# Three half decays at other places in the order of a recurrent attention and mixture kernel, and a gate transpose in four column tiles

## The chip, the cores and the metric

One core of a Trainium2 chip runs the whole program. The metric is the device time of one execution in microseconds (us), taken as the median of several runs. The engines are TensorE (PE in the profile, with PEld for its weight loads), VectorE (DVE), ScalarE (ACT), GpSimd (POOL) and SyncE (SP), which issues the DMAs.

## The reference

A gated recurrent attention (mLSTM) over 2 batches, 8 heads, 768 steps and 40 features, followed by a dense mixture of 4 experts over the 1536 tokens:

```python
m_new = np.maximum(f_gate[:, :, t] + m, i_gate[:, :, t])
f_stab = np.exp(f_gate[:, :, t] + m - m_new)
i_stab = np.exp(i_gate[:, :, t] - m_new)
C = f_stab[:, :, None, None] * C + i_stab[:, :, None, None] * np.einsum('bhd,bhe->bhde', vt, kt)
n = f_stab[:, :, None] * n + i_stab[:, :, None] * kt
h_tilde = np.einsum('bhde,bhe->bhd', C, qt)
nq = np.einsum('bhd,bhd->bh', n, qt)[:, :, None]
y[:, :, t] = sigmoid(o_gate) * h_tilde / np.maximum(np.abs(nq), 1.0)
...
p = domain_probs / (domain_probs.sum(-1, keepdims=True) + 1e-09)
h = np.maximum(x @ w1[e], 0.0)
out += p[:, e:e + 1] * (h @ w2[e])
```

Here x is y with the heads side by side: 320 features for each token. The hidden size is 1024.

## The kernel before

The recurrence is computed in 12 chunks of 128 tokens. Chunk n belongs to batch n % 2 and to position n // 2 of 6. For each chunk the kernel makes score products of keys and queries (`scores`, PE, line L473), weighs them with a matrix of decays (`weigh`, DVE, L479), multiplies with the values (`intra`, PE, L535), adds what the carried state gives (`inter`, PE, L520), normalises (`norm`, DVE, L548 to L555) and transposes the result into the experts' input (`turn`, PE, L562; `turn_lo`, DVE, L573 and L574). `state` (PE, L491) with the additions of L501 (DVE) and `carry` (POOL, L507) bring the state to the next chunk of the batch. `values` (POOL, L456) and `keys` (POOL, L462) scale values and keys; keys needs both halves of the chunk's decays.

`decay(n, i)` (L438) makes half i (4 heads) of the decay matrix of chunk n by one scan on DVE (L442). For chunks 0 to 3 its input fb lies in PSUM, where `spread` put it; from chunk 4 on fb is loaded into SBUF by DMA (`load_f`). Its second input, id4, always lies in SBUF.

The engines run their instructions in the order in which the program issues them, which is written out by hand (manual_schedule). The loop over chunks (L722) issues, for chunk n: state(n), turn_lo(n-1), inter(n+1), intra(n), norm(n), scores(n+1), values, keys, weigh and carry of n+1, and then the steps of `PLAN[n]` (L38): D is the next half of decay n+2, Hjk two hidden tiles of the first expert for 256 tokens (8 times 2 products, L164, then a relu: L207 on ACT for the rounded part, L208 on DVE for the rest), Ojk a quarter of the output products (L224), T the transpose. In chunk 3 the program also issues the last split of the second weight matrix (`split_w2`: L104 on ACT, L107 on POOL), a reciprocal (L761, DVE) and the product of the expert weights with it (L762, POOL), all between carry(4) and the first step of PLAN[3].

The score products and the state and transpose products share the two PSUM buffers of the pool `ps_w`. A new pair of score buffers is free when the state additions (L501) and turn_lo (L573, L574) have read the tiles there before.

`gate_t` (L346) turns the input gates, 48 rows by 128 tokens for each chunk position, to tokens in partitions, with one fp32 product of the whole array for each of the 6 positions (L353): one position early, five later, followed by an ACT copy (L357). An fp32 product shows up as two matrix instructions.

After the 12 chunks the experts run in tiles of 512 tokens, with nothing but products, relus and accumulation.

Of the kernel before, what the change touches and what calls it, by code (L numbers as in the profile page):

```python
# [15 lines left out]
B, H, S, D = 2, 8, 768, 40  # L16
NE, DM, FF = 4, 320, 1024
NT = B * S
L = 128
# [16 lines left out]
NPE = 4  # L36

PLAN = {  # L38
    2: "D H03 D O00 T",
    3: "D O01 D O02 T",  # L40
    4: "D H10 D H11 O03 T",
    5: "D H12 D H13 O10 T",
    6: "D O11 H20 D H21 T",
    7: "D O12 D O13 O20 T",
    8: "D H22 D H23 O21 T",
    9: "D O22 H30 D H31 T",
    10: "O23 H32 H33 O30 T",
    11: "O31 O32 T O33",
}
PAD = 56  # L50

NB = 4
W = 512
# [3 lines left out]
def tile_mlstm_moe(ctx, tc, gt, qk, vk, ot, dp, w1, w2, out):  # L57
    ctx.enter_context(tc.manual_schedule())
    nc = tc.nc

    def pool(name, bufs, **kw):
        return ctx.enter_context(tc.tile_pool(name=name, bufs=bufs, **kw))
# [4 lines left out]
    hps = []  # L67
    pool("pad", 1, side="right").tile([L, PAD], F32, name="pad")
    dram = pool("dram", 1, space=DRAM)
# [58 lines left out]
    def load_w1e(e):  # L128
        raw1 = raws.tile([L, 3, FF], F32, tag="raw", name="raw1")
        nc.sync.dma_start(raw1, w1[e])  # L130
        return raw1
# [111 lines left out]
    with ExitStack() as actx:  # L243
# [40 lines left out]
        ib = gp.tile([L, S], F32, name="ib")  # L284
        fr = a1.tile([L, NPE // B * L], F32R, name="fr")
        f_d = dram.tile([BH, S], F32, name="f_d")
        ident = const.tile([L, L], F32, name="ident")
# [58 lines left out]
        def gate_t(c0, c1):  # L346

            pit = pits[c0] = ps_y.tile([L, 512], F32, tag="y", name="pit")
            n = c1 - c0
            po = n * 48  # L350
            for c in range(c0, c1):
                o = (c - c0) * 48
                nc.tensor.matmul(  # L353
                    pit[:, o:o + 48], ib[:, c * L:(c + 1) * L], ident[:, 0:48],
                    start=True, stop=True,
                )
            nc.scalar.activation(  # L357
                ibT[:, c0:c1], pit[:, 0:po].rearrange("t (c g) -> t c g", c=n), AF.Copy
            )
# [38 lines left out]
        def load_qk(j, c=None):  # L398
            c = slice(0, 2) if c is None else slice(c, c + 1)
            nc.sync.dma_start(qks[j % 2][:, c], qk[j, :, c])  # L400

        def load_vk(j, c=None):
            if j not in vks:
                vks[j] = a2.tile([L, 2, 2, H, D], F32, tag="vk", name="vk")
            c = slice(0, 2) if c is None else slice(c, c + 1)
            nc.sync.dma_start(vks[j][:, c], vk[j, :, c])

        def load_o(j):
            nc.sync.dma_start(acc[:, 2 * j:2 * j + 2], ot[:, 2 * j:2 * j + 2])

        def gate_o(j):
            og = acc[:, 2 * j:2 * j + 2]
            nc.scalar.activation(og, og, AF.Sigmoid)  # L413
# [15 lines left out]
        def load_f(n, fb=None):  # L429
            b, c = n % B, n // B  # L430
            if fb is None:
                fb = a0.tile([L, H, L], F32, tag=f"fb{n % 2}", name="fb")
            fbs[n] = fb[:, 0:4], fb[:, 4:8]
            nc.sync.dma_start(
                fb, f_d[b * H:(b + 1) * H, c * L:(c + 1) * L].unsqueeze(0).to_broadcast([L, H, L])
            )

        def decay(n, i=None):  # L438
            if i != 1:
                dds[n] = a1.tile([L, H, L], F32, tag=f"dd{n % 2}", name="dd")  # L440
            for i in range(2) if i is None else (i,):
                nc.vector.tensor_tensor_scan(  # L442
                    out=dds[n][:, 4 * i:4 * i + 4].rearrange("p h t -> p (h t)"),
                    data0=fbs[n][i].rearrange("p h t -> p (h t)"),
                    data1=id4.rearrange("p h t -> p (h t)"),
                    initial=0.0, op0=ALU.mult, op1=ALU.add,
                )

        def values(n, part=None):
            b, c = n % B, n // B  # L450
            vv = vvs[n] = vp[n % 2]
            iec = ibT[:, c, b * H:(b + 1) * H].unsqueeze(2)
            if part != LO:
                nc.scalar.activation(vv[:, :, D:D + 1], iec, AF.Copy)
            if part != HI:
                nc.gpsimd.tensor_mul(  # L456
                    vv[:, :, 0:D], vks[n // 2][:, n % 2, 0], iec.to_broadcast([L, H, D])
                )

        def keys(n):  # L460
            if n // B < NC - 1:
                nc.gpsimd.tensor_mul(  # L462
                    kp[n % 2], vks[n // 2][:, n % 2, 1],
                    dds[n][:, :, L - 1:L].to_broadcast([L, H, D]),
                )
# [9 lines left out]
        def weigh(n):  # L475
            pms[n] = a1.tile([L, H, L], F32, tag=f"pm{n % 2}", name="pm")
            pm, dd = (t.rearrange("k (p r) t -> k r p t", r=2) for t in (pms[n], dds[n]))
            for r in range(2):
                nc.vector.tensor_mul(pm[:, r], ss[n][r], dd[:, r])  # L479

        def state(n, pool=ps_w, tag="w"):

            b, c, vv, kk = n % B, n // B, vvs[n], kp[n % 2]
            if c == NC - 1:
                return
            st = pool.tile([L, NP, L], F32, tag=tag, name="st")
            blocks = [(slice(64 * r, 64 * r + D), slice(64 * r, 64 * r + D + 1)) for r in range(2)]
            for p in range(NP):
                for r, (q, q2) in enumerate(blocks):
                    h = 2 * p + r  # L490
                    nc.tensor.matmul(  # L491
                        st[q, p, q2], kk[:, h], vv[:, h, 0:D + 1], start=True, stop=True
                    )
            cout = cs[b]
            if c == 0:
                for q, q2 in blocks:
                    copy(nc.scalar, cout[q, :, q2], st[q, :, q2])
            else:
                cd = cds.pop(n)
                for q, q2 in blocks:  # L500
                    nc.vector.tensor_add(cout[q, :, q2], cd[q, :, q2], st[q, :, q2])  # L501
# [29 lines left out]
        def intra(n):  # L531
            y = y0s[n] = ps_y.tile([L, H, 64], F32, tag="y", name="y0")
            for h in range(H):
                for t in (slice(0, 64), slice(64, L)):
                    nc.tensor.matmul(  # L535
                        y[t, h, 0:D + 1], pms[n][:, h, t], vvs[n][:, h, 0:D + 1],
                        start=True, stop=True,
                    )
# [32 lines left out]
        def turn_lo(n):  # L571
            px, t = pxs.pop(n), slice(n * L, (n + 1) * L)
            nc.vector.tensor_sub(xst[:, 3:5, t], px[:, 0:2], xst[:, 0:2, t].bitcast(F32))  # L573
            nc.vector.tensor_sub(xst[C:L, 2, t], px[0:C, 2], xst[0:C, 2, t].bitcast(F32))  # L574
# [147 lines left out]
        for n in range(2, NCH):  # L722
            j, cc = n // 2, n % 2
            plan = PLAN[n].split()
            nxt = n + 1 < NCH
            if cc == 0 and 2 < j + 1 < NG:
                load_qk(j + 1)
                load_vk(j + 1)
            if n > 3 and n + 3 < NCH:
                load_f(n + 3)  # L730
            if cc == 0:
                if j > 1:
                    gate_o(j)
                if j + 1 < NG:
                    load_o(j + 1)
            if n == NCH - 2:
                raw1 = load_w1e(1)
            state(n)
            if n > 2:
                turn_lo(n - 1)  # L740
            if nxt:
                inter(n + 1)
            intra(n)
            norm(n)
            if nxt:
                scores(n + 1)
            for a in plan:
                if a[0] == "H":
                    work[int(a[1])].corners(int(a[2]) // 2 * 4)
                    break  # L750
            if nxt:
                values(n + 1)
                keys(n + 1)
                weigh(n + 1)
                carry(n + 1)
            if n == 2:
                split_w2_lo(w2s, 4, 2, w2r, nc.gpsimd)
            if n == 3:
                split_w2(w2s, 6, 2, w2r, nc.gpsimd)
            if n == 3:  # L760
                nc.vector.reciprocal(psum_e, psum_e)  # L761
                nc.gpsimd.tensor_mul(pw, pw, psum_e.to_broadcast([L, NCH, NE]))  # L762
            half = 0
            for a in plan:
                if a == "T":
                    turn(n, ps_w, "w")
                    turn_d(n, n + 1)
                elif a == "D":
                    decay(n + 2, half)
                    half = 1  # L770
                else:
                    step(a)
# [103 lines left out]
```

## Time and profile before

| | us |
|---|---|
| median of 3 runs | 402.92 (402.8 to 402.92) |
| profiled execution | 402.67 |
| its span | 400.9 |
| PE busy | 395.2 (99%) |
| DVE busy | 172.6 (43%) |
| ACT busy | 127.7 (32%) |
| POOL busy | 81.0 (20%) |

The granted clock of TensorE is at full speed in every slice of the span. A row of a timeline gives the start of an instruction or of a run of equal instructions, its length, engine, line, operation, output and inputs, and in brackets the idle time of the engine before it with what ended it. Consecutive instructions of DVE and POOL overlap a little in the records, so the distance from one start to the next is shorter than the length. The chunks end at about 116 us; the rest of the span is expert work.

### The profile page before, as it was taken

The numbers are of one execution on the slowest core, as the hardware profiler recorded it, in microseconds if no ns is written. First come the engines' busy times: TensorE is split into PE (matmuls) and PEld (weight loads), VectorE is DVE, ScalarE is ACT, GpSimd is POOL, SyncE is SP. The second block draws the span as 40 slices with busy tenths as digits, with TensorE's granted clock in tenths as the row PEclk, the third lists the DMA queues.
The fourth block names the chain that finished last, engine by engine and source line by source line (L and its number), as shares of the span: only waits on it lengthen the run. The fifth ranks groups of instructions, "written<-read, shape, count | busy, mean of one in ns | idle before, by whom it ended". The sixth has DMA issues, their size and how long they took to land.

```text
span 400.9 us, 7146 instructions
## 1 busy us (share of the span) xinstructions
PE 395.2 (99%) x3044; PEld 359.0 (90%) x3044; DVE 172.6 (43%) x313; ACT 127.7 (32%) x309; POOL 81.0 (20%) x93
## 2 busy tenths in 40 slices
PE   9899999999999999999999999999999999999996
PEld 6798999999988988988989989989889889899896
DVE  8878987878534124123133153142241341331321
ACT  4776344444526333016021051061130320220310
POOL 4888622310007110007100010043100100000000
PEclk9999999999999999999999999999999999999999
DMA  6999564670000304000300022003000001001001
GB/s 170 333 299 284 171 156 135 159 289 2 2 0 2 131 2 157 2 0 5 128 0 2 0 70 88 2 1 132 0 0 2 1 2 49 18 14 37 17 18 49
DMA packets 15000, 29.34 MB, mean 73 GB/s; under 512 B 1000, under 2 KB 10760, under 8 KB 13656
## 3 DMA queue, kind: packets, MB, share of 16 engines
q1 hardware_dynamic: 14968, 28.88, 22.7%
q8 instruction: 24, 0.39, 0.4%
q14 instruction: 8, 0.07, 0.1%
HBM read 26.86 MB, written 2.02 MB: 72 GB/s over the span
## 4 chain that ended last, share of the span: by engine, by line
PE 93%; DVE 3%; ACT 2%; POOL 1%; issue 1%; DMA 1%; DVEq 0%; POOLq 0%
PE ph L164 42%; PE po L224 42%; PE s L473 3%; PE y L535 2%; PE y L520 1%; PE px L562 1%; PE st L491 1%; DMA gat<-in_gt 1%; DVE mb L302 0%; PE fb L423 0%; POOL fs L310 0%; ACT yb L527 0%; ACT acc L413 0%; POOL fs L311 0%; POOL ib L321 0%
## 5 line engine op out<-in xcount | busy, mean ns | idle before, releaser
L164 PE MATMUL ph<-xst,w1s 128*128 128x512 f32 (+3 forms) x840 | 174.0, 363 | 0.0
L224 PE MATMUL po<-w2s,h 128*128 128x320 f32 x1152 | 173.2, 310 | 0.0
L224 PEld LDWEIGHTS po<-w2s,h 128*128 128x128 f32 x1152 | 169.8, 188 | 1.5
L164 PEld LDWEIGHTS ph<-xst,w1s 128*128 128x128 f32 (+1 forms) x840 | 141.0, 189 | 28.0 <-issue 4.2
L207 ACT ACTIVATE h<-ph 128x512 fp32r<-128x512 f32 x96 | 57.3, 598 | 198.1 <-PE ph L164 198.1
L208 DVE SCALAR_TENSOR_TENSOR h<-ph,h 128x512 fp32r<-128x512 f32 x96 | 66.1, 689 | 103.4 <-ACT h L207 102.8
L234 DVE SCALAR_TENSOR_TENSOR acc<-po,pw,acc 128x320 f32<-128x320 f32 x36 | 19.8, 551 | 99.9 <-PE po L224 99.9
L107 POOL TENSOR_TENSOR w1s<-raw,w1s 128x512 fp32r<-128x512 f32 (+1 forms) x24 | 23.6, 1023 | 96.7 <-ACT w1s L104 96.7
L107 POOL TENSOR_TENSOR w2s<-raw,w2s 128x640 fp32r<-128x640 f32 x6 | 9.5, 1577 | 98.2 <-ACT w2s L104 98.2
L442 DVE TENSOR_TENSOR_SCAN dd<-fb,id 128x512 f32<-128x512 f32 x22 | 25.9, 1204 | 0.0
L527 ACT ACTIVATE yb<-y,ibT 128x41 f32<-128x41 f32 x80 | 15.9, 316 | 1.0 <-DVE cs L501 0.5
L164 PE MATMUL ph<-xd,w1s 64*128 64x512 f32 (+1 forms) x56 | 15.9, 391 | 0.0
L473 PE MATMUL s<-qk 64*128 64x128 f32 (+1 forms) x192 | 14.9, 284 | 0.5 <-DVE cs L501 0.3
L479 DVE TENSOR_TENSOR pm<-s,dd 128x512 f32<-128x512 f32 x24 | 15.3, 679 | 0.0
L473 PEld LDWEIGHTS s<-qk 64*128 64x128 f32 (+1 forms) x192 | 12.4, 187 | 2.0 <-issue 0.7
L104 ACT ACTIVATE w2s<-raw 128x640 fp32r<-128x640 f32 x12 | 8.8, 734 | 16.6 <-DMA raw<-in_w 16.6
L535 PE MATMUL y<-vp,pm 128*64 128x41 f32 x384 | 13.3, 229 | 0.5 <-POOL vp L456 0.3
L535 PEld LDWEIGHTS y<-vp,pm 128*64 128x64 f32 x384 | 12.6, 138 | 1.0 <-POOL vp L456 0.4
L456 POOL TENSOR_TENSOR vp<-vk,ibT 128x320 f32<-128x320 f32 x12 | 10.5, 876 | 12.7 <-PE y L535 9.5
L462 POOL TENSOR_TENSOR kp<-vk,dd 128x320 f32<-128x320 f32 x10 | 7.3, 736 | 23.7 <-DVE dd L442 23.7
L104 ACT ACTIVATE w1s<-raw 128x512 fp32r<-128x512 f32 (+1 forms) x24 | 11.2, 517 | 0.0
L232 ACT ACTIVATE acc<-po,pw 128x320 f32<-128x320 f32 x12 | 6.3, 528 | 15.1 <-PE po L224 15.1
(86 smaller groups left out, 186.0 us busy)
## 6 DMA issues: line engine op xcount, KB each, us to landing
raw<-in_w SPq DMA_DIRECT2D x3, 1536.0 KB, 9.8
raw<-in_w SPq DMA_DIRECT2D x3, 1280.0 KB, 5.4
fb<-f_d SPq DMA_DIRECT2D x7, 512.0 KB, 4.9
qk<-in_qk SPq DMA_DIRECT2D x4, 832.0 KB
vk<-in_vk SPq DMA_DIRECT2D x5, 640.0 KB, 10.2
acc<-in_ot SPq DMA_DIRECT2D x6, 320.0 KB, 9.5
out<-acc SPq DMA_DIRECT2D x12, 160.0 KB, 1.8
qk<-in_qk SPq DMA_DIRECT2D x4, 416.0 KB
```

The source lines that it names most:

```text
L104: nc.scalar.activation(hi, raw, AF.Copy)
L107: eng.tensor_sub(lo, raw, hi.bitcast(F32))
L164: nc.tensor.matmul(self.banks[i][:, f % self.nf, :], self.w1s[r, wi, f * L:(f + 1) * L], x[r, self.t0:self.t0 + self.n], start=(i not in s ...
L207: nc.scalar.activation(hh, ph, AF.Relu)
L208: nc.vector.scalar_tensor_tensor(out=hl, in0=ph, scalar=0.0, in1=hh.bitcast(F32), op0=ALU.max, op1=ALU.subtract)
L224: nc.tensor.matmul(po, self.hs[f][a][:, sl], ws[:, b, f, :], start=(first and i == 0), stop=(last and i == len(ks) - 1),)
L234: nc.vector.scalar_tensor_tensor(out=acc[:, i, :], in0=po, scalar=pw[:, i, e:e + 1], in1=acc[:, i, :], op0=ALU.mult, op1=ALU.add,)
L442: nc.vector.tensor_tensor_scan(out=dds[n][:, 4 * i:4 * i + 4].rearrange("p h t -> p (h t)"), data0=fbs[n][i].rearrange("p h t -> p (h t)") ...
L473: nc.tensor.matmul(ss[n][r][:, p, :], kg[q, p], qg[q, p], start=True, stop=True)
L479: nc.vector.tensor_mul(pm[:, r], ss[n][r], dd[:, r])
L527: nc.scalar.activation(yb[:, h], y1[:, h, 0:D + 1], AF.Copy, scale=ibT[:, c, i:i + 1])
L535: nc.tensor.matmul(y[t, h, 0:D + 1], pms[n][:, h, t], vvs[n][:, h, 0:D + 1], start=True, stop=True,)
```

## The change

The second half of the decay of chunk 4 is issued in chunk 3, between values(4) and keys(4), instead of in chunk 2. The second halves of chunks 8 and 11 are issued ahead of a hidden step (H20, H30) instead of after it. Each of the six products of gate_t becomes four, with 32 tokens each, that write 32 partitions of the result.

```diff
 PLAN = {
-    2: "D H03 D O00 T",
+    2: "D H03 O00 T",
...
-    6: "D O11 H20 D H21 T",
+    6: "D O11 D H20 H21 T",
...
-    9: "D O22 H30 D H31 T",
+    9: "D O22 D H30 H31 T",
...
+QUADS = [slice(i, i + 32) for i in range(0, L, 32)]
...
-                nc.tensor.matmul(
-                    pit[:, o:o + 48], ib[:, c * L:(c + 1) * L], ident[:, 0:48],
-                    start=True, stop=True,
-                )
+                for t in QUADS:
+                    nc.tensor.matmul(
+                        pit[t, o:o + 48], ib[:, c * L + t.start:c * L + t.stop],
+                        ident[:, 0:48], start=True, stop=True,
+                    )
...
                 values(n + 1)
+                if n == 3:
+                    decay(4, 1)
                 keys(n + 1)
```

## Rows read from the trace of the kernel before

**Rows 1.** The page, section 1: busy time, share of span, instructions of each engine.
```profile
PE 395.2 (99%) x3044; PEld 359.0 (90%) x3044; DVE 172.6 (43%) x313; ACT 127.7 (32%) x309; POOL 81.0 (20%) x93
```
**Rows 2.** The chain that ended last, in order of time: start us, us, what.
```profile
38.62 0.30 DVE xst L574
38.91 0.04 issue
38.95 1.16 PE s L473 x14
```
**Rows 3.** Timeline of PE, chunks 3 and 4.
```profile
35.84 0.51 PE L491 MATMUL st<-vp,kp 128*40 128x41 f32 x16
36.92 1.08 PE L535 MATMUL y<-vp,pm 128*64 128x41 f32 x32
...
45.16 1.08 PE L535 MATMUL y<-vp,pm 128*64 128x41 f32 x32
46.17 1.16 PE L473 MATMUL s<-qk 64*128 64x128 f32 x16
```
**Rows 4.** Timeline of DVE over the same stretch.
```profile
34.59 1.28 DVE L442 TENSOR_TENSOR_SCAN dd<-acc,id 128x512 f32<-128x512 f32 x1
...
36.38 1.21 DVE L442 TENSOR_TENSOR_SCAN dd<-acc,id 128x512 f32<-128x512 f32 x1
37.51 0.64 DVE L501 TENSOR_TENSOR cs<-cd,st 40x164 f32<-40x164 f32 x2
...
38.62 0.28 DVE L574 TENSOR_TENSOR xst<-px,xst 64x128 fp32r<-64x128 f32 x1
38.82 0.49 DVE L548 TENSOR_TENSOR y<-y,yb 128x328 f32<-128x328 f32 x1
...
40.81 1.28 DVE L479 TENSOR_TENSOR pm<-s,dd 128x512 f32<-128x512 f32 x2
...
42.14 2.31 DVE L442 TENSOR_TENSOR_SCAN dd<-fb,id 128x512 f32<-128x512 f32 x2
44.70 0.66 DVE L501 TENSOR_TENSOR cs<-cd,st 40x164 f32<-40x164 f32 x2 [0.26 <-PE st L491]
...
46.29 0.51 DVE L548 TENSOR_TENSOR y<-y,yb 128x328 f32<-128x328 f32 x1 [0.17 <-PE y L535]
```
**Rows 5.** Timeline of POOL over the same stretch.
```profile
33.21 1.59 POOL L107 TENSOR_TENSOR w2s<-w2r,w2s 128x640 fp32r<-128x640 f32 x1
34.74 1.66 POOL L456 TENSOR_TENSOR vp<-vk,ibT 128x320 f32<-128x320 f32 x1
37.73 0.74 POOL L462 TENSOR_TENSOR kp<-vk,dd 128x320 f32<-128x320 f32 x1 [1.34 <-DVE dd L442]
38.42 1.04 POOL L507 TENSOR_TENSOR cd<-cs,bl 104x512 f32<-104x512 f32 x1
39.52 1.56 POOL L107 TENSOR_TENSOR w2s<-w2r,w2s 128x640 fp32r<-128x640 f32 x1
42.30 1.06 POOL L762 TENSOR_TENSOR pw<-pw,psum_e 128x48 f32<-128x48 f32 x1 [1.22 <-DVE psum_e L761]
43.33 1.63 POOL L456 TENSOR_TENSOR vp<-vk,ibT 128x320 f32<-128x320 f32 x1
```
**Rows 6.** The tile vp, its products on POOL: length ns min/median/max.
```profile
L456 POOL TENSOR_TENSOR vp<-vk,ibT x12: 712/722/1655, 10.7 to 92.1; 128x320 f32<-128x320 f32 x12
```
**Rows 7.** Timeline of DVE: two halves of a decay in chunk 7, with POOL idle.
```profile
76.84 2.33 DVE L442 TENSOR_TENSOR_SCAN dd<-fb,id 128x512 f32<-128x512 f32 x2
```
**Rows 8.** Timelines of PE, DVE and ACT around the end of chunk 6.
```profile
73.37 1.57 PE L473 MATMUL s<-qk 64*128 64x128 f32 x16
...
71.74 0.67 DVE L208 SCALAR_TENSOR_TENSOR h<-ph,h 128x512 fp32r<-128x512 f32 x1
...
71.06 0.60 ACT L207 ACTIVATE h<-ph 128x512 fp32r<-128x512 f32 x1 [1.08 <-PE ph L164]
```
**Rows 9.** The chain that ended last: pieces of small fp32 products, with their counts.
```profile
22.82 0.74 PE st L491 x32
...
24.60 1.10 PE pit L353 x10
...
45.33 0.91 PE y L535 x32
```

## The prediction

> **What bounds the kernel now.** I read first the busy table of the page: PE is busy for 99% of the span [rows 1], so an edit pays only where it removes a PE gap or PE work, and costs where it makes PE wait. Next the chain that ended last. It is PE almost everywhere from 17 us on, except for one stretch up to 38.95 us that runs through DVE: there the score products of chunk 4 (PE, L473) wait for the second turn_lo subtraction of chunk 2 (DVE, L574) [rows 2]. Last I read the timelines of PE, DVE and POOL around that place, row by row, since an edit that moves DVE work must be followed there.
>
> The size of that gap: the y products (L535) of chunk 3 start at 36.92. In the next chunk the scores start 1.01 us after the y products (45.16 to 46.17) [rows 3], so these could start at 37.93. Their second product starts at 38.95. PE loses 1.02 us. The reason is on DVE [rows 4]: the second half of decay 4 runs from 36.38 to 37.59, then come the state additions (37.51) and turn_lo (to 38.90), and only then are both score buffers of ps_w free.
>
> One chunk on, PE does not wait, but only just: DVE ends turn_lo(3) a moment before the scores of chunk 5 start at 46.17. DVE is idle there for 0.26 us (before 44.70) and 0.17 us (before 46.29) [rows 3, 4]. So DVE between 34.59 and 46.3 has about 0.4 us to spare in all, and a DVE instruction of 1.13 us that is moved inside that stretch can't vanish.
>
> **Part 1, decay(4,1) moved from chunk 2 to chunk 3.** It leaves the place after H03's relu and stands between norm(3) and weigh(4). It issues no DMA. Removed: DVE goes from 36.38 straight to the state additions, which must wait for PE's state products (35.84 + 0.51 = 36.35), so about 36.45; additions and turn_lo take 1.39 us (37.51 to 38.62 + 0.28) [rows 3, 4], so the buffers are free at 37.85, before PE wants them at 37.93. The gap of 1.02 us is gone, and PE reaches the scores of chunk 5 at 46.17 - 1.02 = 45.15.
>
> Added, in DVE's order: norm(3) starts when its y products are in, 36.92 + 1.13 (the lag 45.16 to 46.29) = 38.05. norm takes 1.99 (38.82 to 40.81): 40.04. The moved half: next instruction after 1.13 (36.38 to 37.51), end after 1.21: 41.17 and 41.25. weigh(4) and the reciprocal, 1.33 (40.81 to 42.14): decay(5,0) is due at 42.50. If nothing disturbs the two halves of decay 5, they take 2.31 less the 0.08 overlap: 44.73; additions and turn_lo 1.39: 46.12; the scores follow 0.05 later (38.90 to 38.95): 46.17 [rows 2 to 4]. That is exactly the old time. So even undisturbed **the 1.02 us come back as a wait one chunk later**: net 0.0 us. What is late next is the scores of chunk 5, behind cs and turn_lo.
>
> And it is disturbed, by POOL. Queued behind the new wait on POOL are keys(4), carry(4), the last low-part split of w2 (L107), the pw product (L762) and values(5). Before, keys, carry and split ran at 37.73, 38.42 and 39.52, while DVE was at norm and weigh, and POOL was idle when decay 5 began [rows 5]. Now keys(4) starts 0.14 us after the decay's end (37.59 to 37.73): 41.39; carry(4) 0.69 later: 42.08, until 43.12; the split right behind it. Carry and split now fall on the two scans of decay 5 (due 42.50).
>
> What do such neighbours cost? A scan of a chunk from 4 on has both inputs in SBUF (fb loaded by DMA, id4). Values(4) on POOL took 1.66 us and values(5) 1.63, where the median of this product is 0.72; both began during such a scan [rows 4 to 6]. Taking 0.72 off the end of the first (36.40) leaves 35.68: POOL stood still until 0.19 us before the scan's recorded end (35.87). The other way round there is one row: decay(4,0) began while the POOL split of 33.21 was running and took 1.28 instead of 1.21 [rows 4, 5]; so it began in fact 0.07 later, at 34.66, 0.14 before that split's end (34.80). A running POOL instruction holds a scan of this kind, and a running scan holds POOL. Who goes first between two scans: L762 began at 42.30, in the first scan of decay 5, and ended at 43.36, while the second scan ran until 44.45 [rows 4, 5], so a waiting POOL instruction gets in between. It was short (48 columns), and that pair took 2.31 against 2.33 for a pair with POOL idle [rows 4, 7], so this row can't show what a long one costs.
>
> The sum by this: decay(5,0) is held from 42.50 to 43.12 - 0.14 = 42.98 and ends at 44.19. The split gets in at 44.19 - 0.19 = 44.00 and takes 1.56: 45.56. decay(5,1) runs from 45.56 - 0.14 = 45.42 to 46.63. The additions start 0.08 before that, 46.55; turn_lo ends 47.94; scores at 47.99 instead of 46.17: **+1.82 us** on PE. Bounds: 0.0 if the two engines don't hold each other; +0.48 if only carry holds a scan. I take the upper end, since three POOL rows and one DVE row are lengthened by it. Afterwards PE and DVE are late by nearly the same, and in later chunks POOL waits for the decay anyway, so no second clash follows.
>
> The Trainium skill, "SBUF — State Buffer", section "Who interferes with whom", states that a DVE instruction with two SBUF inputs and a GpSimd instruction that reads SBUF take an exclusive lock, and that the second to issue is blocked for the whole instruction of the first. Here it speaks against the change: by it alone, both carry and split would hold the scans, which is the sum just made; without it the sum would be zero.
>
> **Part 2, decays 8 and 11.** The second half now runs before the relu of H20 (H30) instead of after it, in DVE time that was idle. In chunk 6 the DVE half of the H21 relu started at 71.74, but ACT's half ended only at 71.06 + 0.60 = 71.66 [rows 8]. So what follows moves up by at most 0.08, and I take 0.05. The next scores on PE, those of chunk 8, wait 0.41 us (1.57 against 1.16 for the 16) [rows 3, 8], and that wait stays nearly whole. keys(8) runs earlier on POOL while DVE has no scan. Chunk 9 shows the same pattern without a wait: 0. If the idle time were too short, the first relu would be late by a few hundredths, still under its successor.
>
> **Part 3, the gate turn.** 12 matrix pieces (two for each chunk's fp32 product) become 48, of 32 output rows each; 40 of them lie at 24.6 us, where PE has no gap. Before: 1.10 us for 10. No row has 32-column pieces. The nearest: 64-column pieces with 41 moving columns, 0.91 / 32 = 28 ns; 40-column pieces, 0.74 / 32 = 23 ns [rows 9]. At 28 ns: 40 x 28 = 1.14, a loss of 0.04. At 23: 0.92, a gain of 0.18. If four tiles overlap twice as well as two: 0.46, a gain of 0.64. I take the nearest in width, 0.18. ACT's reading of the result doesn't bind. The other 8 pieces stand in the start-up, where PE runs filler products: 0.
> The skill's page "TensorEngine Tiling (Array Packing)", section "Performance Considerations", gives some 60 cycles of overhead to each matmul; that would be an estimate of 25 ns a piece at 2.4 GHz, 1.0 us for 40, a gain of 0.1. No row here has this width.
>
> **The sum**, against the profiled execution (402.67 us, span 400.9): +1.82 - 0.05 - 0.18 = +1.59, 404.26. The median of the timed runs is 0.25 higher, 402.92, so **404.5**. What a measurement of this kernel can tell from no change is about 0.2%, 0.8 us.
>
> **The rivals.**
> A, the forecast: carry and split hold the scans. 404.5, with the bounds of the gate turn 404.0 to 404.7. For it: the lengthened rows. Against: only one DVE row is lengthened, and by 0.07 only. Chance 0.53.
> B: carry holds the first scan, but the second scan follows the first before the split gets in (DVE's next instruction is already queued). +0.48 - 0.23 = +0.25: 403.2. For it: the pair of decay 5 was not lengthened by L762. Chance 0.18.
> C, the other side: DVE is not held by POOL, POOL alone waits. Then the gap goes from the scores of chunk 4 to those of chunk 5 and the change does not do what its first edit is after; only the gate turn counts: 0.0 - 0.23: 402.7 (402.2 to 402.9). It decides as soon as decay 5 stays at 2.3 us a pair. Chance 0.22.
> D: as C, with the 32-column pieces at half of 23 ns or less, so that 0.64 or more comes off PE and the DVE chain moves up with it: about 402.1 or below. Chance 0.07; I count most of it as faster by over 0.2%.
>
> Faster by over 0.2%: 0.06; within: 0.40 (B, C, the rest of D); slower: 0.54 (A and a little of B). For 8 in 10 the range must reach into C: 402.5 to 404.9, where the upper end adds to A's 404.7 a few hundredths for each of its hand-overs; A's own is 404.0 to 404.7.
>
> **What would show it.** Right: no gap before the scores of chunk 4; a DVE pair of decay 5 that spans some 4 us instead of 2.31, with a POOL split between its halves, and a gap of nearly 3 us before the scores of chunk 5. Wrong: decay 5 at 2.3 us (C), or only its first half long (B). Part 3 is read from the start of the gate pieces to the next hidden products (1.10 before), part 2 from the scores' 1.57. The prediction falls most likely if a waiting scan is served ahead of POOL, or if POOL's order differs from the one that I read.

## The result and the profile after

The changed kernel takes 407.32 us (median of 4 runs, 406.12 to 408.79) against 402.92 for the kernel before: slower by a ratio of 1.0092, 95% interval 1.0065 to 1.0119 (that of the two medians is 1.0109). The profiled execution took 407.58 us, its span is 405.8.

The page shows the busy table with PE at 98% [rows 1], and in the line of the granted clock two slices below 9, which the kernel before does not have:

```profile
PE 398.7 (98%) x3080; PEld 361.9 (89%) x3080; DVE 175.2 (43%) x313; ACT 127.8 (31%) x309; POOL 81.1 (20%) x93
...
PEclk9999889999999999999999999999999999999999
```

PE's timeline over chunks 3 and 4 [rows 3]:

```profile
38.11 1.26 PE L475 MATMUL s<-qk 64*128 64x128 f32 x16
...
44.42 1.08 PE L537 MATMUL y<-vp,pm 128*64 128x41 f32 x32
47.77 2.32 PE L475 MATMUL s<-qk 64*128 64x128 f32 x14 [2.27 <-DVE cs L503]
...
50.86 5.14 PE L165 MATMUL ph<-xst,w1s 128*128 128x256 f32 x28
55.84 1.93 PE L225 MATMUL po<-w2s,h 128*128 128x320 f32 x12
```

The scores of chunk 4 (38.11) take 1.26 us, 0.10 more than the 1.16 of [rows 3]: their old gap is all but gone. The first score product of chunk 5 waits 2.27 us, and the others wait for turn_lo (DVE below, 48.09 + 0.28 = 48.37): the forecast gap of nearly 3 us is there. What was not forecast stands in the lengths behind that: 16 scores that took 1.16 us [rows 3] take over 2, and 28 hidden products take 5.14. In the kernel before they took 3.62:

```profile
47.50 3.62 PE L164 MATMUL ph<-xst,w1s 128*128 128x256 f32 x28
50.96 1.34 PE L224 MATMUL po<-w2s,h 128*128 128x320 f32 x8
```

DVE and POOL over the same stretch [rows 4, 5]:

```profile
40.23 1.22 DVE L444 TENSOR_TENSOR_SCAN dd<-acc,id 128x512 f32<-128x512 f32 x1
41.55 1.29 DVE L481 TENSOR_TENSOR pm<-s,dd 128x512 f32<-128x512 f32 x2
...
42.90 4.17 DVE L444 TENSOR_TENSOR_SCAN dd<-fb,id 128x512 f32<-128x512 f32 x2
46.99 0.64 DVE L503 TENSOR_TENSOR cs<-cd,st 40x164 f32<-40x164 f32 x2
...
48.09 0.28 DVE L576 TENSOR_TENSOR xst<-px,xst 64x128 fp32r<-64x128 f32 x1
```
```profile
41.59 0.74 POOL L464 TENSOR_TENSOR kp<-vk,dd 128x320 f32<-128x320 f32 x1 [4.82 <-DVE dd L444]
42.30 1.04 POOL L509 TENSOR_TENSOR cd<-cs,bl 104x512 f32<-104x512 f32 x1
43.30 1.55 POOL L108 TENSOR_TENSOR w2s<-w2r,w2s 128x640 fp32r<-128x640 f32 x1
44.80 1.19 POOL L766 TENSOR_TENSOR pw<-pw,psum_e 128x48 f32<-128x48 f32 x1
45.95 1.63 POOL L458 TENSOR_TENSOR vp<-vk,ibT 128x320 f32<-128x320 f32 x1
```

The pair of decay 5 spans 4.17 us instead of 2.31 [rows 4]. Carry and split have their usual lengths, stand together and end at 44.85, in its first half; the pw product and values(5) behind them are the stretched ones.

The stretches around the gap; the columns are the stretch, its length, the busy time of PE, PEld, DVE, ACT and POOL with the count of instructions, the granted clock, the share of the DMA engines and GB/s:

```profile
44.00:46.00 2.00, 1.50 (x46) 1.38 (x42) 2.00 (x2) 1.96 (x8) 2.00 (x3) 1.00 0.01 5
46.00:48.00 2.00, 0.23 (x1) 0.26 (x2) 1.96 (x4) 0.68 (x5) 2.00 (x2) 0.89 0.00 0
48.00:50.00 2.00, 2.00 (x16) 1.81 (x18) 1.85 (x8) 0.00 (x0) 1.95 (x3) 0.50 0.72 210
...
54.00:56.00 2.00, 2.00 (x18) 2.00 (x17) 1.11 (x2) 0.60 (x1) 0.00 (x0) 0.91 0.00 0
56.00:58.00 2.00, 2.00 (x16) 1.82 (x14) 1.36 (x2) 1.32 (x3) 1.15 (x2) 1.00 0.00 0
```

From 48 to 54 us the granted clock is 0.50, the lower of the two levels, 1.2 GHz. So the 4.9 us between the two spans are in two places. The scores of chunk 5 start at 47.77 instead of 46.17: 1.60. From there to the output products of chunk 4 (55.84; 50.96 in the kernel before, whose chain then runs on without a wait) it takes 8.07 us instead of 4.79: 3.28. All that follows is equal to 0.01 us.

The gate turn and what stands behind it, in PE's timeline, with keys(2) from POOL's:

```profile
24.91 0.63 PE L355 MATMUL pit<-ident,ib 128*32 128x48 f32 x40
25.47 1.94 PE L165 MATMUL ph<-xst,w1s 128*128 128x256 f32 x14
...
28.81 0.51 PE L493 MATMUL st<-vp,kp 128*40 128x41 f32 x16
```
```profile
28.02 0.74 POOL L464 TENSOR_TENSOR kp<-vk,dd 128x320 f32<-128x320 f32 x1
```

From the first gate piece to the next hidden products it is now 0.56 us for 40 pieces, 14 ns a piece. The state products of chunk 2 then start at 28.81, right at the end of keys(2) (28.76); in the kernel before they started at 28.72. This execution had begun its hidden products later (17.98 against 17.62); counted from there, 0.27 us of the saving is left at the state products (10.83 us against 11.10), but on the time line nothing is.

The wait before the scores of chunk 8 is 0.03 us shorter than in [rows 8]:

```profile
78.25 1.54 PE L475 MATMUL s<-qk 64*128 64x128 f32 x16
```

### The profile page after: what moved, and what is told of

It is laid out like the page before. It is cut to its first block, busy times and chain, and to the rows that moved or that the text cites. A ratio compares the mean times of both kernels' runs of the same rounds, so it can differ in the third digit from the quotient of the medians.

```text
span 405.8 us, 7218 instructions
## 1 busy us (share of the span) xinstructions
PE 398.7 (98%) x3080; PEld 361.9 (89%) x3080; DVE 175.2 (43%) x313; ACT 127.8 (31%) x309; POOL 81.1 (20%) x93
## 4 chain that ended last, share of the span: by engine, by line
PE 96%; DVE 3%; issue 1%; DVEq 0%
PE ph L165 43%; PE po L225 41%; PE s L475 3%; PE y L537 2%; PE pwm L85 2%; PE y L522 2%; PE fb L425 1%; PE px L564 1%; PE st L493 1%; DVE dd L444 1%; DVE pm L481 1%; DVE xr L557 0%; DVE xr L554 0%; PE pit L355 0%; DVE cs L503 0%
## 5 line engine op out<-in xcount | busy, mean ns | idle before, releaser
L165 PE MATMUL ph<-xst,w1s 128*128 128x512 f32 (+3 forms) x840 | 176.0, 366 | 0.0
L165 PEld LDWEIGHTS ph<-xst,w1s 128*128 128x128 f32 (+1 forms) x840 | 142.7, 191 | 28.2 <-issue 4.4
L444 DVE TENSOR_TENSOR_SCAN dd<-fb,id 128x512 f32<-128x512 f32 x22 | 27.6, 1288 | 0.1
L475 PE MATMUL s<-qk 64*128 64x128 f32 (+1 forms) x192 | 16.1, 297 | 2.3 <-DVE cs L503 2.3
L475 PEld LDWEIGHTS s<-qk 64*128 64x128 f32 (+1 forms) x192 | 13.5, 198 | 3.7 <-issue 2.7
```

The lines of the kernel that those rows point to most:

```text
L165: nc.tensor.matmul(self.banks[i][:, f % self.nf, :], self.w1s[r, wi, f * L:(f + 1) * L], x[r, self.t0:self.t0 + self.n], start=(i not in s ...
L444: nc.vector.tensor_tensor_scan(out=dds[n][:, 4 * i:4 * i + 4].rearrange("p h t -> p (h t)"), data0=fbs[n][i].rearrange("p h t -> p (h t)") ...
L475: nc.tensor.matmul(ss[n][r][:, p, :], kg[q, p], qg[q, p], start=True, stop=True)
```

## The experiments

**Theory 1**: POOL's carry and split hold the scans of decay 5, PE stands still for over 2 us, and TensorE works at 1.2 GHz for some us behind that. **Rivals**: the other parts have a share in the loss; the low clock is no result of the gap; DVE is late for a reason other than POOL. Each ratio below is against runs of the kernel before on the same chip, whose medians there were 403.1 to 403.5 us; it is not that of the two medians.

### e1: without the move of decay 4

```diff
-    2: "D H03 O00 T",
+    2: "D H03 D O00 T",
...
-                if n == 3:
-                    decay(4, 1)
```

> The changed kernel with decay(4,1) back at its old place in chunk 2; decays 8 and 11 and the gate turn stay changed. Theory 1 (the moved half of decay 4 causes the whole loss: POOL's carry and split hold the two scans of decay 5, PE stands still for over 2 us before the scores of chunk 5, and TensorE then runs at 1.2 GHz for some us): decay 5 takes 2.3 us as a pair, PE waits about 1 us before the scores of chunk 4 and not at all before those of chunk 5, the clock stays at its upper level, 402.3 to 403.0 us. Rival (the 32-column pieces or the two other moved halves cost something, since the trace of after starts its hidden products 0.36 us later): 403.5 us or more.

404.22 us median (402.80 to 406.18), ratio 1.0013 (0.9982 to 1.0043). Most of the loss is gone, but the median misses theory 1's range and lies in the rival's, and the ratio can't tell this kernel from the one before; e2 decides between the two. The time scatters more than either theory said, and the profiled execution (405.12 us) shows one reason. The first half of decay 4, PE, and the stretch behind:

```profile
35.25 1.53 DVE L444 TENSOR_TENSOR_SCAN dd<-acc,id 128x512 f32<-128x512 f32 x1 [0.62 <-DMA acc<-f_d]
```
```profile
39.20 0.46 PE L475 MATMUL s<-qk 64*128 64x128 f32 x2 [1.26 <-DVE cs L503]
```
```profile
40.00:42.00 2.00, 2.00 (x16) 1.78 (x17) 1.86 (x7) 0.00 (x0) 1.87 (x2) 0.58 0.93 206
```

Decay 4 waited for its transfer. The old gap before the scores of chunk 4 was longer than in the profile of before, and the clock fell behind it. The kernel before scatters in the same way: among 34 of its runs on one chip (that of e5 to e10), 24 took 402.70 to 404.29 us at a mean granted clock of 0.998 to 1.0, and 10 took 404.96 to 405.93 at 0.995 to 0.998.

### e2: the move of decay 4 alone

```diff
-    2: "D H03 D O00 T",
+    2: "D H03 O00 T",
...
                 values(n + 1)
+                if n == 3:
+                    decay(4, 1)
```

> The kernel before with decay(4,1) moved, nothing else. Theory 1: the pair of decay 5 spans about 4.2 us, the scores of chunk 5 wait over 2 us, the granted clock falls to the lower level behind that wait and the time is 406 to 409 us, as with the whole change. Rival (the other parts have a share in it): 403 to 405.5 us.

407.43 us (405.39 to 408.56), ratio 1.0061 (1.0030 to 1.0093). The pair of decay 5 spans 4.17 us again, PE waits 2.36 us before the scores of chunk 5, and the clock falls to 0.50. The move alone makes the loss, as far as the two intervals tell; the rival falls.

### e3: the gap filled

```diff
+            if n == 4:
+                for _ in range(3):
+                    keep_warm(512)
             if nxt:
                 scores(n + 1)
```

> The changed kernel with three filler products of 512 columns on zeros, which nobody reads, before the scores of chunk 5, so that PE works while it would stand still. Theory 1 splits the loss of 4.9 us into 1.6 us by which the scores of chunk 5 come later and 3.3 us in which PE works at 1.2 GHz behind the gap. With the gap filled the second share goes: no slice at the lower clock, 404.2 to 405.2 us, while the pair of decay 5 still spans about 4.2 us. Rival (the low clock doesn't come from PE standing still, or the slow stretch behind the gap is something else, as a wait of the hidden products): no gain, or a loss of the fillers' 2.5 us: 407 to 410 us.

405.49 us (404.58 to 407.12), ratio 1.0045 (1.0020 to 1.0070); span 403.3. PE, the last turn_lo subtraction on DVE, and the stretches:

```profile
44.63 1.08 PE L537 MATMUL y<-vp,pm 128*64 128x41 f32 x32
45.65 2.85 PE L85 MATMUL pwm<-const-float32-0.0 128*128 128x512 f32 x6
48.43 1.16 PE L475 MATMUL s<-qk 64*128 64x128 f32 x14
...
49.90 3.62 PE L165 MATMUL ph<-xst,w1s 128*128 128x256 f32 x28
```
```profile
48.23 0.28 DVE L576 TENSOR_TENSOR xst<-px,xst 64x128 fp32r<-64x128 f32 x1
```
```profile
48.00:50.00 2.00, 2.00 (x23) 1.44 (x21) 1.87 (x7) 0.00 (x0) 2.00 (x3) 1.00 0.76 220
```

DVE is as late as before (pair 4.17 us, from 43.04), PE still can't go on sooner, but it works meanwhile on zeros, and the clock stays at its upper level; all 10 runs have a mean clock of 0.999 or more. The 28 hidden products behind the scores take 3.62 us again instead of 5.14. On the same chip the medians of e2 and e3, 407.43 and 405.49, put the price of the low clock at nearly 2 us; the profiled spans of the changed kernel and e3 (405.8 and 403.3) put it at 2.5. The expectation of 404.2 to 405.2 was a little low: its 1.6 us was read at the first score product, but the others wait for turn_lo, which ends at 48.51, and the hidden products start 2.40 us later than before (49.90 against 47.50). What makes the slowest of these runs (up to 407.12) slow at full clock is not shown.

### e4: POOL's work ahead of the moved half

```diff
                 if n == 3:
+                    split_w2_lo(w2s, 6, 2, w2r, nc.gpsimd)
+                    carry(4)
                     decay(4, 1)
                 keys(n + 1)
                 weigh(n + 1)
-                carry(n + 1)
+                if n != 3:
+                    carry(n + 1)
...
```

> The changed kernel with POOL's split and carry(4) issued ahead of the moved half, where POOL has nothing to do (ACT's part of the split goes one chunk earlier for that), so that neither runs during decay 5. Theory 1: the pair of decay 5 takes 2.3 us again, the scores of chunk 5 start within 0.3 us of the kernel before (46.2), the clock stays up, 402.3 to 403.1 us. Rival (DVE is late for another reason, as a transfer of fb or the order of the scans): the pair stays above 3.5 us and the time above 405 us.

403.59 us (403.23 to 406.67), ratio 1.0015 (0.9987 to 1.0042). DVE, PE and POOL of its profile:

```profile
34.51 2.23 DVE L444 TENSOR_TENSOR_SCAN dd<-acc,id 128x512 f32<-128x512 f32 x1
...
43.22 2.31 DVE L444 TENSOR_TENSOR_SCAN dd<-fb,id 128x512 f32<-128x512 f32 x2
```
```profile
46.23 0.46 PE L475 MATMUL s<-qk 64*128 64x128 f32 x2 [0.24 <-DVE cs L503]
46.89 0.94 PE L475 MATMUL s<-qk 40*128 40x128 f32 x12 [0.21 <-DVE xst L576]
...
48.22 3.62 PE L165 MATMUL ph<-xst,w1s 128*128 128x256 f32 x28
```
```profile
34.92 0.73 POOL L458 TENSOR_TENSOR vp<-vk,ibT 128x320 f32<-128x320 f32 x1
```

With carry and split out of the way the pair is back at 2.31 us (the short pw product falls into it as in the kernel before): these two were what held DVE. All ten runs lie above the expected 402.3 to 403.1 us. The first score product of chunk 5 starts at 46.23 against 46.17 before, but the others wait for turn_lo until 46.89, and the hidden products start 0.72 us late (48.22 against 47.50). Most of that comes from another place: the scan of decay(4,0), due at 34.51, took 2.23 us, because values(4) went ahead of it, and so norm(3) began at 38.57 instead of 36.84 + 1.13 = 37.97, 0.60 late. Without that some 0.1 us would be left, an estimate. That an undisturbed move only carries the wait one chunk on, the forecast's "net 0.0", is near this but was not run by itself.

### e5: only the split ahead, carry left behind keys

> The changed kernel with only POOL's split ahead of the moved half; carry(4) stays behind keys(4) and so at the start of decay 5. If a running POOL instruction holds a scan for as long as it runs and no longer: the pair of decay 5 takes 2.31 + 0.5 = 2.8 us, the scores of chunk 5 wait 0.7 to 1.1 us, the clock stays up, 403.0 to 404.2 us. Rival (the hold is all or nothing, or another POOL instruction takes the split's place between the scans): the pair stays above 3.5 us, 405 us or more.

The edit is that of e4 without its carry line. 405.79 us (404.35 to 408.73), ratio 1.0061 (1.0035 to 1.0087). DVE's pair and POOL:

```profile
43.09 3.35 DVE L444 TENSOR_TENSOR_SCAN dd<-fb,id 128x512 f32<-128x512 f32 x2
```
```profile
42.49 1.04 POOL L509 TENSOR_TENSOR cd<-cs,bl 104x512 f32<-104x512 f32 x1
43.49 1.19 POOL L766 TENSOR_TENSOR pw<-pw,psum_e 128x48 f32<-128x48 f32 x1
44.63 0.72 POOL L458 TENSOR_TENSOR vp<-vk,ibT 128x320 f32<-128x320 f32 x1
```

3.35 us, not 2.8, and the time and the clock missed the expectation too: in 7 of the 12 runs the mean clock is 0.996 or less. Carry holds the first scan for some 0.4 (43.09 to 43.53). Between the scans, by the lengths, not one POOL instruction got in but two, pw and values(5), the latter at its unhindered 0.72. The rival's "another POOL instruction takes the split's place" was right in kind. Which of them get in is not settled by the runs: in the changed kernel values(5) stood behind pw in the same way, but waited for the second scan (1.63).

### e8 and e9: the wait handed on to chunk 6

The second halves of decays 5, 6 and 7 were also moved one chunk later, with carry and the loads arranged for it; e9 also put values(2), keys(2) and carry(2) ahead of a split, and the relu of H03 ahead of decay 4.

```diff
+LAG = (3, 4, 5, 6)
...
+                if n in LAG:
+                    carry(n + 1)
+                    decay(n + 1, 1)
+                    if n > 3:
+                        load_f(n + 3)
```

> The changed kernel with the second halves of decays 5, 6 and 7 each moved one chunk later in the same way as that of 4, carry and split ahead of them on POOL, and the loads of fb 7 to 9 behind them. If the wait before the scores of chunk 5 is DVE's amount of work in one chunk, passing it on to chunk 6, where DVE stands idle for over 1 us, removes it: no PE wait over 0.3 us before the scores of chunks 4 to 7, 401.5 to 402.6 us. Rival (each chunk is as full as the one before, so the wait only moves on): waits of 0.5 to 1 us before the scores of chunks 6 or 7 and 402.8 to 404 us.

405.03 us (402.88 to 408.13), ratio 1.0041 (1.0010 to 1.0071).

> As e8_lag, and in chunk 2 the relu of H03 goes ahead of the first half of decay 4 (which then can wait 0.6 us longer for its transfer), and values(2), keys(2) and carry(2) go ahead of the first low part of w2 on POOL, so that the state products of chunk 2 no longer wait for keys(2). If the 0.54 us that the 32-column pieces save are lost in that wait: the state products of chunk 2 start 0.2 to 0.4 us sooner against the end of the gate pieces than in the changed kernel, and 401.0 to 402.3 us. Rival (another wait is right behind it): no sooner, and the time of e8_lag.

404.97 us (402.75 to 407.74, and one run of 409.08 that the ratio leaves out), ratio 1.0015 (0.9984 to 1.0045). Neither kernel reached the times expected. In the profile of e8 the waits before the scores of chunks 5 to 7 are gone, as the theory had it, but the time is not better: the trouble had moved ahead of chunk 4. That profile is of one of the quicker runs (403.62 us); what the slower ones waited for is not shown. DVE's first half of decay 4 and POOL's values(4) in e8:

```profile
35.23 2.13 DVE L445 TENSOR_TENSOR_SCAN dd<-acc,id 128x512 f32<-128x512 f32 x1
```
```profile
35.55 0.72 POOL L459 TENSOR_TENSOR vp<-vk,ibT 128x320 f32<-128x320 f32 x1
```

The scan, due at 35.23, let values(4) pass and took 2.13. In e9's profile its transfer landed 0.86 us late and values(2) had waited 2.73 us for vk, so its second question, whether keys(2) eats the gate turn's saving, stayed unanswered there.

### e10 and e12: the scatter of the kernel before

e10 puts one filler of 512 columns before the scores of chunk 4; e12 queues the load for decay 4 ahead of the second load of vk.

```diff
+            if n == 3:
+                keep_warm(512)
             if nxt:
                 scores(n + 1)
```
```diff
-        load_vk(2)
         load_f(NPE, acc[:, 8:12].rearrange("p c d -> p (c d)")[:, 0:H * L]
                .rearrange("p (h t) -> p h t", h=H))
+        load_vk(2)
```

> The kernel before with one filler product of 512 columns (0.85 us) in its own gap before the scores of chunk 4. If the scatter of the kernel before (402.8 to 407.8 us) comes from that gap, which is longer when the transfer for decay 4 lands late, and from TensorE working at 1.2 GHz behind it: nearly all runs at 402.8 to 404.0 us. Rival (the scatter is from elsewhere, as the start-up): the same scatter, up to 406 us and more.

403.62 us (402.84 to 408.25), ratio 0.9990 (0.9963 to 1.0017). 11 of the 12 runs lie at 402.84 to 403.68 with a clock of 0.999 or more; one, at 408.25, does not. In the profile, of a run of 403.49 us, decay 4 waited 0.45 us for its transfer, and the clock stayed up all the same.

> The kernel before with the load for decay 4 queued ahead of the second load of vk instead of behind it. If the scatter of the kernel before comes from decay 4 waiting for its transfer: decay(4,0) never waits for the DMA, nearly all runs at 402.7 to 403.2 us. Rival (the gap is long by POOL holding the scan, or the loads behind it come late in turn): the same scatter, up to 405 us and more.

402.94 us (402.71 to 405.01), ratio 0.9991 (0.9974 to 1.0008). 11 of 12 runs at 402.71 to 403.53. The profiled one, 405.01 us, has no wait for the DMA, but the rival's cause:

```profile
34.70 1.97 DVE L442 TENSOR_TENSOR_SCAN dd<-acc,id 128x512 f32<-128x512 f32 x1
```
```profile
34.88 0.71 POOL L456 TENSOR_TENSOR vp<-vk,ibT 128x320 f32<-128x320 f32 x1
```
```profile
39.09 0.46 PE L473 MATMUL s<-qk 64*128 64x128 f32 x2 [0.97 <-DVE cs L501]
```

So both a late transfer (e1) and values(4) passing the scan lengthen the old gap. How much of the scatter they make is not shown: neither ratio is clear of 1, and one run in twelve above 404.9 us, here and in e10, stands against 3 of 29 and 10 of 34 of the kernel before on the same chips, too few to tell a change of the spread.

### e11 and e13: every decay one chunk later

In e11 both halves of every decay from chunk 4 on stand ahead of weigh, with split and carry ahead of them on POOL. e13 is the same with the gate turn of the kernel before.

```diff
-    3: "D O01 D O02 T",
+    3: "O01 O02 T",
...
+                carry(n + 1)
+                if n > 2:
+                    decay(n + 1)
+                    if 3 < n < NCH - 3:
+                        load_f(n + 3)
                 keys(n + 1)
                 weigh(n + 1)
-                carry(n + 1)
```

> A kernel built from what the runs showed: both halves of every decay from chunk 4 on stand between norm(n) and weigh(n+1), one chunk later than in the kernel before; POOL's carry and split are issued ahead of them, keys behind them. No scan is left between the scores of chunk 3 and those of chunk 4, decay 4 is needed at 40 us instead of 34.6, and POOL has nothing to run during a scan. By the theory of the lock and of the gap: no PE wait over 0.3 us before the scores of chunks 4 and 5, clock at its upper level in nearly all runs, 401.4 to 402.4 us. Rival (weigh and with it the y products now come too late, since a decay of 2.3 us stands before it): waits of PE before the y products or the state products of chunks 4 to 10, 403 us or more.

402.36 us (402.17 to 403.61), ratio 0.9977 (0.9962 to 0.9992): below the kernel before and the changed one. PE, DVE and POOL of its profile:

```profile
37.91 1.16 PE L475 MATMUL s<-qk 64*128 64x128 f32 x16
...
43.21 0.55 PE L564 MATMUL px<-ident,xr 128*128 128x128 f32 x3 [0.42 <-DVE pm L481]
...
45.99 1.16 PE L475 MATMUL s<-qk 64*128 64x128 f32 x16
```
```profile
40.03 2.33 DVE L444 TENSOR_TENSOR_SCAN dd<-acc,id 128x512 f32<-128x512 f32 x2
42.46 1.29 DVE L481 TENSOR_TENSOR pm<-s,dd 128x512 f32<-128x512 f32 x2
```
```profile
43.97 0.27 POOL L767 TENSOR_TENSOR pw<-pw,psum_e 128x48 f32<-128x48 f32 x1 [0.79 <-DVE psum_e L766]
```

No wait before the scores of chunks 4 and 5. The rival has a part: the transpose of chunk 3 now waits some 0.4 us for weigh(4), whose score buffer it takes. Most of the 1.02 us goes there: from the output products behind the scores of chunk 4 to the state products it takes 4.89 us (39.01 to 43.90), 4.04 in the kernel before (40.04 to 44.08). What is left is the gain, and a clock of 0.999 or more in all 12 runs.

> As e11_late with the gate turn of the kernel before (10 pieces of the whole array instead of 40 of 32 columns). The pieces themselves took 0.56 us against 1.10. If that saving reaches the end: 0.3 to 0.5 us above e11_late. Rival (it is lost in the wait of the state products of chunk 2 for keys(2)): within 0.15 us of e11_late.

402.61 us (402.42 to 403.01), ratio 0.9980 (0.9967 to 0.9994). 0.25 us above e11, between the two expectations, with intervals that overlap; in the two profiles the transpose of chunk 3 stands at 43.53 and 43.21. Counted from the start of the hidden products (17.73 and 17.86), that transpose comes 0.45 us sooner with the new gate turn. So most of what the pieces save can pass on; the medians show about half of the 0.54, and the runs do not settle it closer.

## Why the prediction was wrong

**The sign and the mechanism were right.** The gap before the scores of chunk 4 went, came back before those of chunk 5, and POOL's carry and split made it long. e2 shows that it is this edit alone, e4 that it is carry and split on POOL. The forecast pair of decay 5, 42.50 to 46.63, is 4.13 us; measured 4.17.

**The step that failed is the sum's first term, "+1.82 us on PE".** It counted a gap of nearly 3 us of TensorE, which the prediction named, at its length alone, at 2.4 GHz behind it. The gap measured 2.27 us up to the first score product, and turn_lo, for which the others wait, ended at 48.37 where the sum had 47.94. Then the granted clock fell to 0.50, and PE paid 3.28 us more for the next stretch, some of it the rest of the wait. e3, which fills the gap, keeps 2.40 us of the 4.88 and gives 2 to 2.5 us back while DVE stays late: that part is the clock's price. Nothing in the sum or the range stood for it, so the range ended at 404.9. The Trainium skill, "TensorE: Matmul & The Clock Gate", section "HAM oscillation — how this bites in real kernels", describes a kernel whose waits for DMA throttle TensorE, so that the work after each wait starts at the lower clock; for a wait on DVE this trace agrees (0.23 us of PE work from 46 to 48, then 0.50). The gap of the kernel before, in whose profile the clock held, was no proof that a longer one costs only its length: in e1 (1.26 us) and e12 (0.97 us up to the first score product) the clock fell behind it (0.58 from 40 to 42 us in e1).

**Smaller misses in the same term.** The scans were due at 42.50 and began at 42.90. 0.19 of it is the moved half itself: weigh(4) reads its result and started 1.32 us after it (40.23 to 41.55), where the forecast took 1.13, the distance to an instruction that doesn't depend on the scan. Another 0.18 is norm(3), at 38.23 instead of 38.05, since the y products of chunk 3 began 0.18 later in this execution (37.10 against 36.92). The order on the two engines was another than forecast, by the lengths: the first scan did not get in between carry and split, but waited for both, and pw went between the scans. That the pair came out at the forecast length all the same is luck.

**Rivals.** B (only carry holds) was near nothing that ran: e5, made for it, gave 3.35, not 2.8. C's first condition, that POOL does not hold DVE, falls with the pair of 4.17 us; its statement that the wait only moves by a chunk is near what e4 shows with carry and split away, after the estimate made there. D falls with C's condition; its gate pieces of half of 23 ns or less came near (14 ns).

**Part 2** was right: 1.57 became 1.54. **Part 3** was mis-sized in the pieces (0.18 forecast, 0.54 measured, inside the bounds) and wrong in the rest of its sentence: that "PE has no gap" there does not mean that a gain passes on. keys(2) ended at 28.76 and the state products could not start sooner. Counted from the products ahead of the pieces (23.87; 23.50 in the kernel before), the hidden products behind them come after 1.60 us instead of 2.03, a saving of 0.43 rather than 0.54, of which 0.27 is left at the state products. The later start of PE's hidden products (17.98 against 17.62) looks like scatter: the eight profiles with the new gate turn have 17.63 to 17.98, the five with the old one 17.62 to 17.73; its cause was not tested.

**The scatter** was not in the forecast at all: it read one execution of the kernel before in which the transfer for decay 4 had landed in time.

## What to carry to other kernels

Price a PE gap in two terms: its length, and the stretch behind it at half the clock; the second can be as large as the first, and a filler product in the gap is a cheap way to measure it. When an instruction with two SBUF inputs is moved on VectorE, look at what GpSimd has ready at the new place, and move that out of the way with it. Moving work inside a stretch where the engine has no idle time moves the wait; here even moving every chunk's decay by one place (e11) left most of it at another place, and gained about 0.2%.

## What the runs showed of the hardware

A VectorE scan with two SBUF inputs and a GpSimd instruction that reads SBUF exclude each other whichever came first: the pw product took 0.27 us alone (e11), 1.19 behind a scan; a pair of scans took 2.31 alone and 4.17 with two GpSimd instructions of 1.04 and 1.55. The Trainium skill, "SBUF — State Buffer", section "Who interferes with whom", says that whoever issues first gets the ports for the whole instruction; the runs agree for the one that runs, but not for the queue behind it: a scan that was already due saw the next GpSimd instruction go first (the split behind carry in the changed kernel, after 0.4 us; values(4) in e4, e8 and e12, after 0.2 to 0.4), while in the kernel before the scan went ahead of the same values(4) [rows 4, 5]. No order among those that wait follows from these runs.

Forty fp32 pieces of 32 columns took 14 ns each, half of what 64-column pieces took (28 ns in [rows 9]). The Trainium skill, "TensorEngine Tiling (Array Packing)", section "Performance Considerations", states some 60 cycles of overhead for each matmul, an estimated 25 ns at 2.4 GHz; these pieces, in four column tiles that may have overlapped, lie below it.
